# Seven-part product 3, LayerNorm sums on ScalarE, and an earlier order of small work, in a two-layer linear-attention and GLU kernel

## The chip, the cores and the metric

One core of one Trainium2 chip. The metric is the device time of one execution in microseconds (us). Besides the time, each run has a span, from its first to its last instruction; it is 1.7 to 2.1 us shorter than the time.

## The reference, cut to what matters

```python
# x: 2048 x 1024; wqkv: 1024 x 3072; w_gate, w_up: 1024 x 3584; w_down: 3584 x 1024; bf16
x = x + A(layernorm(x))      # linear attention, 32 heads
x = x + B(layernorm(x))      # B(x) = ((x @ w_gate) * (x @ w_up)) @ w_down
x = x + A(layernorm(x))      # the same weights again
x = x + B(layernorm(x))
```

## The kernel before

Large products are made from seven smaller ones, numbered 1 to 7, of sums of quarter matrices (the Strassen scheme in a form with eight sums, S1 to S4 of one operand and T1 to T4 of the other). Each of the two layers has two passes of gate/up and "down", a pass for each half of the tokens. Within "down" some of the seven products are split once more, into seven parts with sums of their own; `L2DOWN` says which, and `DSCHED` after which group of matmuls each sum is put on VectorE.

```python
L2DOWN = {(False, 0): "45", (False, 1): "5", (True, 0): "45", (True, 1): "453"}   # (second layer?, pass): split products
DSCHED = {
    ...
    "5": {"20": "S1:5", "21": "S2:5", "22": "S3:5", "23": "S4:5", "41": "T1:5", "42": "T2:5", "43": "T3:5", "5d": "T4:5"},
    "453": {... "5d": "T4:5 S4:3", "5h": "T1:3", "5k": "S3:3", "5m": "T2:3", "3d": "T3:3", "3f": "T4:3"},
}
```

Every operation names the pages that it reads and writes, and the program works out its waits from that; each engine runs its operations in the order of the program. LayerNorm of a tile of 128 tokens takes its sums on VectorE (`ln_a`) or, for five tiles of the first LayerNorm, on ScalarE in two steps (`ln_s1`, `ln_s2`) with a little GpSimd arithmetic after each; then comes the standardisation (`ln_b2`) and a transposing DMA from SBUF to SBUF. The standardised tile lies in a buffer:

```python
def dst(self, n):                      # buffer of the n-th tile
    if self.to == "A0":
        return xrt[n], r_xr(n)
    o = (O_XN + [O_WQ])[n % 3] if self.to == "B" and n < 14 else O_XN[n % 2]    # B: three in turn, two for the last tiles
    return vh(o, D), R(o, D * 2)

def start(self, i, mid=None):
    if self.to == "A0" and i in LN_ACT:
        j = ln_s1(self.order[i], *self.dst(i))       # ScalarE: sum
        self.q_s.append((i, j))                      # squares follow in s2()
    else:
        j = ln_a(self.order[i], mid)                 # VectorE: bn_stats, bn_aggr
    ...

def lnstep(i, h):                      # first projections, one tile behind another
    if h == 0:
        ...
        if lnp.n < NST:
            lnp.start(lnp.n)
        lnp.b_one()
    else:
        lnp.s2()
        ...

def p7(c):                             # gate/up: bank of product 7, copied, then the multiply of the finished quarter
    pe("7", c, X[c], False)
    cp(1, c, X[c])
    c22(c)
```

Of the kernel before, what the change touches and what calls it, by code (L numbers as in the profile page):

```python
# [180 lines left out]
def build_kernel(nc, A_x, A_wqkv, A_wo, B_w_gate, B_w_up, B_w_down, out):  # L181
    _, S, D = A_x.shape
# [20 lines left out]
    ORDER0 = "D3A' P1A P7B' P6A D2B' 51 D4B' D3B' R0 56 D2A P1B T0 P7A 57 P5A W P6B T1 D4A R0 P5B S5+"  # L203
    ORDER1 = "P5A' 47' T0 P7B' D4A' P5B' 11 D3A' R0 51 16 D4B' D2B' P1A 17 T1 56 D3B' P6A P1B 41 R0 57 S5+ S2+ D2A P6B 46 P7A"
    ORDER2 = "11 57' D2B' P7B' 16 T0 P5A' 21 D4B' P1A 17 S2+ D3A' P5B' 26 R0 P6A D2A S5+ 41 27 P1B D3B' 46 51 T1 P7A 47 P6B 56 D4A R0"
    L2DOWN = {(False, 0): "45", (False, 1): "5", (True, 0): "45", (True, 1): "453"}
    DSCHED = {
        "45": {"20": "S1:5 S1:4", "21": "S2:5 S2:4", "22": "S3:5 S4:4", "23": "S4:5", "70": "S3:4 T1:4", "72": "T2:4 T3:4", "73": "T1:5",
               "4d": "T4:4", "4j": "T2:5", "4m": "T3:5", "5d": "T4:5"},
        "5": {"20": "S1:5", "21": "S2:5", "22": "S3:5", "23": "S4:5", "41": "T1:5", "42": "T2:5", "43": "T3:5", "5d": "T4:5"},  # L210
        "453": {"20": "S1:5 S1:4", "21": "S2:5 S2:4", "22": "S3:5 S4:4", "23": "S4:5", "70": "S3:4 T1:4", "71": "S1:3", "72": "T2:4 T3:4", "73": "T1:5",
                "4d": "T4:4", "4f": "S2:3", "4j": "T2:5", "4m": "T3:5", "5d": "T4:5 S4:3", "5h": "T1:3", "5k": "S3:3", "5m": "T2:3", "3d": "T3:3", "3f": "T4:3"},
    }
    ORDERS = {(False, 0): ORDER0, (False, 1): ORDER1, (True, 0): ORDER2, (True, 1): ORDER2}
    SZ_W = KT * D * 2
# [109 lines left out]
    with ExitStack() as es:  # L325
# [13 lines left out]
        def vh(o, n):  # L339
            return ah[:, o // 2: o // 2 + n]  # L340
# [158 lines left out]
        class LN:  # L499
# [13 lines left out]
            def dst(self, n):  # L513
# [2 lines left out]
                o = (O_XN + [O_WQ])[n % 3] if self.to == "B" and n < 14 else O_XN[n % 2]  # L516
                return vh(o, D), R(o, D * 2)

            def start(self, i, mid=None):
                assert i == self.n  # L520
                if self.to == "A0" and i in LN_ACT:
                    j = ln_s1(self.order[i], *self.dst(i))
                    self.q_s.append((i, j))
                else:
                    j = ln_a(self.order[i], mid)
                self.n += 1
                self.q_b.append((i, j))

            def s2(self, upto=NST):
                while self.q_s and self.q_s[0][0] <= upto:  # L530
                    i, j = self.q_s.pop(0)
                    ln_s2(self.order[i], j, *self.dst(i))

            def b1_one(self):
                if self.q_b:
# [368 lines left out]
        def layer_A(lnp, nxt, first):  # L904
# [173 lines left out]
            def lnstep(i, h):  # L1078
                if h == 0:
                    if first and lnp.n < NST:  # L1080
                        for t in range(lnp.n, lnp.n + 5):
                            if xnext[0] <= t < NST:
                                xload(t)
                                xnext[0] = t + 1
                    if lnp.n < NST:
                        lnp.start(lnp.n)
                    lnp.b_one()
                else:
                    lnp.s2()
                    lnp.use_dma = i + 1 >= NPE_T  # L1090
                    lnp.step_t(1)
# [20 lines left out]
                seq += [("q", i - NHOLD - 1), ("k", i)]  # L1112
            seq += [("q", i) for i in range(max(NPL - NHOLD - 1, 0), NPL if NPL < NST else 0)]
            mids = {("k", 2, 0): lambda: None}
            lead = [[], [lambda: lnp.step_t(1)], [lambda: lnp.start(4)], [lambda: lnp.b_one(), lambda: lnp.start(5)]]
            if first:
                (p0, e0_), (p1_, e1_) = [proj("k", tok[0], h, "parts") for h in range(2)]
                (pt1, et1), (pt1b, et1b) = [proj("k", tok[1], h, "parts") for h in range(2)]
# [259 lines left out]
        def layer_B(lnp, nxt, first):  # L1378
# [10 lines left out]
            def pair(ps_, p, l2):  # L1389
# [66 lines left out]
                def p7(c):  # L1456
                    pe("7", c, X[c], False)
                    cp(1, c, X[c])
                    c22(c)

                def p5(c):
                    if "5" in L:
# [2 lines left out]
                        pe("5", c, Y[c], True)  # L1465
                    c22(c)

                ORDER = [q[0] for q in ORDERS[not first, ps_].split() if q[0] in "1245" and q[1] == "1"]

                def l2_of(q):  # L1470
# [103 lines left out]
                def fin(q, c):  # L1574
# [4 lines left out]
                        pe(q, c, bank, False)  # L1579
                    add = L[q]["s"](c) if q in L and q in "24" else cpb(0, c) if q == "3" else None  # L1580
                    return lambda: mul(c, {"2": "1", "4": "4", "3": "3"}[q], bank, add)
                return dict(p1=p1, p5=p5, p6=p6, p7=p7, L=L, fin=fin, sums=sums)

            def gateup(ps_, ticks, l2):
                jit = first and ps_ == 0
# [28 lines left out]
                                return  # L1614

                def emit(p, tk, head=False):
                    if tk[-1] == "'":
                        p, tk = p - 1, tk[:-1]
                    if p < 0 or (p == 0 and not head and tk in pre):
                        return  # L1620
                    if p == 1 and tk[0] in l2 and tk[1] == "1":
                        tp_next(tk[0])
                    c, x = pairs[p], "AB".find(tk[-1])
                    if tk[0] == "P":
                        c["p" + tk[1]](x)
                    elif tk[0] == "D":
                        c["fin"](tk[1], x)()
                    elif tk[0] in "1245":
                        step(p, tk[0], int(tk[1]))
                    elif tk[0] == "R":  # L1630
                        if p or tk == "R1":
                            ring_issue()
                    elif tk == "W":
                        wd_dma()
                    elif tk[0] == "S" and not (early and p == 0):
                        sums(p + (tk[2] == "+"), tk[1])
                    elif tk[0] == "T":
                        i = int(tk[1])
                        if jit:
                            store_s(n0 + 2 * p + i)  # L1640
                            if p + 1 < NP:
                                prep_s(n0 + 2 * p + 2 + i)
                        ticks(2 * p + i)
                    if p == 0 and tk in ("P1B", "P5B", "D2B", "D4B") and tk[1] in l2:
                        plain.add(tk[1])
                    if p == 0 and not head:
                        tp_next()
# [32 lines left out]
            def down(ps_, ticks, tail):  # L1680
# [12 lines left out]
                    i = i0 + 4 * sh + t  # L1693
                    return x_res[:, i, d * 512:(d + 1) * 512], r_x(i, d * 512, (d + 1) * 512)

                def final(sh, d, t):
                    i = i0 + 4 * sh + t
                    if is_last:
                        xs, rx = xq(sh, d, t)
                        dma(out2[i * 128:(i + 1) * 128, d * 512:(d + 1) * 512], xs, [], KOUT, rd=rx)  # L1700

                def hblk(q, kh, mh):
                    hv, ho = hs[q]
# [12 lines left out]
                    return xnT[:, 0:7, c0:c0 + 256], _seg(O_XT, 7, S * 2, c0 * 2, (c0 + 256) * 2)  # L1716

                tr, ha_ = [flat(O_T + 3584 * i) for i in range(3)], [flat(O_HA + 3584 * i) for i in range(4)]
                sbuf2 = {"4": [xbuf(i) for i in range(3)], "5": tr if "4" in l2d else [xbuf(1 + i) for i in range(3)], "3": [xbuf(i, 1 - ps_) for i in range(3)]}
                tbuf2 = {"4": [flat(RE), flat(RE + 3584), flat(O_XN[0])], "5": [xbuf(3) if "4" in l2d else ha_[2], ha_[0], ha_[1]], "3": [ha_[2], ha_[3], xbuf(3, 1 - ps_)]}  # L1720
                r4 = [(vf(o, 512), R(o, 2048)) for o in (RC, RC + 2048, RB + 28672, RB + 30720)]
                l2w = {}
                for q in l2d:
# [17 lines left out]
                def run_l2(q, evac):  # L1741
# [49 lines left out]
                    def m7(r):  # L1791
                        mm(7, r, UB[r], 1)
                        if q == "5":
                            put5(r + 2, r)
                            put(r + 2, r)
                        else:
                            acc(r + 2, 1, r, 1, rout)
                            acc(r + 2, 0, r, 1, rin)

                    def m2(r):  # L1800
                        mm(2, r, DB[r], 0)
# [4 lines left out]

                    def m4(r):
                        mm(4, r, DB[r + 2], 0)
                        evac(r + 2)
                    f = first_  # L1810
                    order = ((f, 0), (f, 1), (m2, 0), (m6, 0), (m2, 1), (m6, 1), (m7, 0), (m3, 0), (m7, 1), (m3, 1), (m4, 0), (m4, 1))
                    for st_, (fn, r) in enumerate(order):
                        fn(r)
                        if st_ == 9:
                            ring_issue()
                            ring_issue()
                        l2_ops(q, "abcdefghijkm"[st_])

                tail(0)
                for qi, q in enumerate(DPROD):  # L1820
# [106 lines left out]
            def dticks1(q, t):  # L1927
                if is_last:
                    return
                if q != "3":  # L1930
                    nxt.step_t(1)
                    nxt.b2_one()
                    nxt.b1_one()
                    if t % 2 == 0 and nxt.n < 8:
                        nxt.start(nxt.n)
                if q == "1" and t == 3:
                    for c in (1, 2, 4):
                        tw_load("k", c)
                if q == "7" and t == 3:
                    for c in (2, 4):  # L1940
                        tw_load("q", c)
                if q == "5":
                    s_make(nxt.order, 0)[t]()
                if q == "5" and t == 3:
                    for w in "kq":
                        load_w(w, 0)
                        t, v, c0, base = WSRC[w]
                        dma(t[:, 4:8, 512:1024], v[:, 4:8, c0 + 512:c0 + 1024], _seg(base + 4 * D * 2, 4, D * 2, 1024, 2048), KW[w][1])
                        tw_load(w, 3)
                    tw_load("q", 1)  # L1950
                if q == "3":
                    stash(12 + t)
                    nxt.step_t(1)
                    nxt.b2_one()
                    nxt.b1_one()
                    nxt.start(8 + t)
                    if t == 3:
                        for k in range(4):
                            stash(8 + k)
# [81 lines left out]
```

## Time and profile before

| | before |
|---|---|
| time, median of 3 (range) | 1434.42 us (1434.38 to 1434.63) |
| span of the profiled run | 1432.5 us |
| TensorE busy | 99% |
| VectorE, ScalarE, GpSimd busy | 84%, 48%, 10% |
| the waits of TensorE that the prediction lists, from start to start | 6.0 us in all |

The prediction shows the lines behind this.

### The profile page before, as it was taken

How to read it: one execution, taken by the hardware profiler on the slowest of the kernel's cores; microseconds unless marked ns; L12 is line 12 of the kernel's file. 1: busy time of each engine (PE TensorE's matmuls, PEld its weight loads, DVE VectorE, ACT ScalarE, POOL GpSimd, SP SyncE). 2: the span in 40 equal slices, each digit the busy share in tenths (PEclk: the TensorE clock that was granted, in tenths of full speed). 3: DMA queues (queue and kind: packets, MB, share of what 16 DMA engines can do in the span).
4: the chain of work that ended last, by engine and by line, in shares of the span. 5: the costliest groups of instructions: out<-in, count | busy, mean ns of one | idle time of the engine just before them, and what ended most of it. 6: DMA issues, size and time to landing. Idle time of an engine off the chain costs nothing.

```text
span 1432.5 us, 21777 instructions
## 1 busy us (share of the span) xinstructions
PE 1420.4 (99%) x8107; PEld 786.5 (55%) x8167; DVE 1210.1 (84%) x2371; ACT 687.8 (48%) x1409; POOL 148.5 (10%) x181
## 2 busy tenths in 40 slices
PE   9999999999999999999999999999999999999999
PEld 4444444555546566664544444446666475666547
DVE  6897878999988799988679978778888887888888
ACT  5882355444410266652157814667766004767400
POOL 2203521000010000002000045300000100000000
PEclk9999999999999999999999999999999999999999
DMA  7868979997786777768793366767775976777653
GB/s 231 208 141 230 222 173 199 305 308 265 253 265 215 228 258 249 251 227 308 225 291 92 90 173 167 176 187 254 260 246 193 292 254 225 259 259 260 204 192 120
DMA packets 270554, 320.73 MB, mean 224 GB/s; under 512 B 164080, under 2 KB 210928, under 8 KB 270448
## 3 DMA queue, kind: packets, MB, share of 16 engines
q1 hardware_dynamic: 270448, 319.34, 72.9%
q8 instruction: 64, 1.05, 0.3%
q14 instruction: 42, 0.34, 0.1%
HBM read 236.45 MB, written 73.40 MB: 216 GB/s over the span
## 4 chain that ended last, share of the span: by engine, by line
PE 86%; DVE 8%; ACT 2%; issue 2%; DMA 1%; POOL 1%; SPq 0%; POOLq 0%; DVEq 0%
PE ps L1414 28%; PE ps L1495 17%; PE ps L1831 14%; PE ps L1230 8%; PE ps L1332 6%; PE ps L970 6%; PE ps L1749 5%; DVE arena L802 4%; DVE arena L454 1%; PE ps L943 1%; DVE arena L805 1%; DMA arena<-arena 1%; DVE arena L649 1%; ACT arena L662 1%; PE ps L1256 1%
## 5 line engine op out<-in xcount | busy, mean ns | idle before, releaser
L802 DVE TENSOR_TENSOR arena<-arena 128x512 f16<-128x512 f16 (+9 forms) x1019 | 499.2, 518 | 59.5 <-ACT arena L1499 34.1
L1414 PE MATMUL ps<-arena 128*128 128x512 f16 x1888 | 457.0, 379 | 0.5 <-DVE arena L805 0.4
L805 DVE SCALAR_TENSOR_TENSOR arena<-ps,arena 128x512 f16<-128x512 f32 (+3 forms) x545 | 353.9, 664 | 67.5 <-PE ps L1831 28.4
L1495 PE MATMUL ps<-arena 128*128 128x256 f16 x2184 | 287.6, 273 | 1.0 <-DVE ps L1508 1.0
L1414 PEld LDWEIGHTS ps<-arena 128*128 128x128 f16 (+1 forms) x1888 | 182.9, 98 | 162.9 <-ACT ps L1443 3.8
L1495 PEld LDWEIGHTS ps<-arena 128*128 128x128 f16 (+1 forms) x2184 | 212.0, 98 | 91.9 <-ACT arena L1499 7.1
L1831 PE MATMUL ps<-arena 128*128 128x512 bf16 (+1 forms) x1102 | 242.6, 379 | 0.9
L1831 PEld LDWEIGHTS ps<-arena 128*128 128x128 f16 x1120 | 109.5, 98 | 130.3 <-DVE arena L802 0.3
L1419 ACT ACTIVATE arena<-ps 128x512 f32<-128x512 f32 x224 | 133.8, 597 | 76.4 <-PE ps L1414 61.6
L1499 ACT ACTIVATE arena<-ps 128x256 f32<-128x256 f32 x351 | 125.1, 384 | 26.9 <-PE ps L1495 22.0
L970 PE MATMUL ps<-arena 128*128 128x512 f16 (+1 forms) x606 | 134.1, 379 | 1.1 <-ACT arena L977 0.4
L1230 PE MATMUL ps<-arena 128*128 128x512 bf16 x498 | 114.7, 379 | 0.7
L1332 PE MATMUL ps<-arena 128*128 128x512 bf16 x502 | 110.3, 379 | 0.5
L459 POOL TENSOR_SCALAR arena<-arena 128x1 f32<-128x1 f32 x59 | 20.8, 353 | 805.4 <-DVE arena L458 805.4
L1505 ACT COPY ps<-ps 128x256 f32<-128x256 f32 x182 | 66.3, 364 | 75.4 <-DVE arena L805 30.0
L970 PEld LDWEIGHTS ps<-arena 128*128 128x128 f16 x616 | 59.5, 98 | 74.7 <-ACT arena L977 5.8
L1443 ACT COPY ps<-ps 128x512 f32<-128x512 f32 x112 | 65.4, 584 | 63.2 <-PE ps L1414 51.9
L1072 POOL TENSOR_TENSOR arena<-arena 128x1024 f16<-128x1024 f32 x32 | 77.0, 2405 | 155.9 <-DVE arena L1070 142.6
L1749 PE MATMUL ps<-arena 128*128 128x256 f16 (+1 forms) x784 | 86.7, 273 | 0.7 <-DVE arena L805 0.5
L454 DVE BATCH_NORM_STATS2 arena<-arena 128x6 f32<-128x512 bf16 x118 | 81.2, 688 | 5.0 <-DMA arena<-in_A_x_dram 3.0
L1508 DVE TENSOR_TENSOR ps<-ps,arena 128x256 f32<-128x256 f32 x182 | 76.7, 428 | 10.3 <-PE ps L1495 9.4
L1332 PEld LDWEIGHTS ps<-arena 128*128 128x128 f16 x512 | 50.1, 98 | 60.4
(72 smaller groups left out, 939.8 us busy)
## 6 DMA issues: line engine op xcount, KB each, us to landing
arena<-w_scratch SPq DMA_DIRECT2D x84, 896.0 KB, 4.5
arena<-t_scratch SPq DMA_DIRECT2D x32, 896.0 KB, 5.7
arena<-in_B_w_down_dram SPq DMA_DIRECT2D x24, 896.0 KB, 5.1
arena<-sp_scratch SPq DMA_DIRECT2D x26, 768.0 KB, 4.3
w_scratch<-arena SPq DMA_DIRECT2D x28, 512.0 KB, 6.1
arena<-w_scratch SPq DMA_DIRECT2D x28, 384.0 KB, 4.9
x_scratch<-arena SPq DMA_DIRECT2D x40, 256.0 KB, 7.3
arena<-x_scratch SPq DMA_DIRECT2D x40, 256.0 KB, 5.8
```

The costliest lines, as they stand in the source:

```text
L454: P.add("dve", (lambda h: lambda e: e.bn_stats(st[j][:, 6 * h:6 * h + 6], x_res[:, i, (D // 2) * h:(D // 2) * (h + 1)]))(h), rd=r_x(i, (D ...
L802: P.add("dve", lambda e: e.tensor_tensor(out=out, in0=a, in1=b, op=op), rd=rd, wr=wr, prd=prd)
L805: P.add("dve", lambda e: e.scalar_tensor_tensor(out=out, in0=a, scalar=sc, in1=b, op0=ALU.mult, op1=op1), rd=rd, wr=wr, prd=prd)
L970: P.add("pe", lambda e: [e.matmul(psb(bank), a[0][:, k, :], b[0][:, k, :], start=(q in (1, 5) and k == 0), stop=(k == 3), skip_group_check ...
L1230: return [e.matmul(psb(bank), xrt[t][:, jj * 128:(jj + 1) * 128], pk[:, h, t, :], start=(t == tok[0]), stop=(t == tok[NST - 1])) for t in ts]
L1332: return [e.matmul(psb(bank), xnT[:, g, i * 128:(i + 1) * 128], wp[:, g, dh * 512:(dh + 1) * 512], start=(dh == 0 and g == 0), stop=(g == ...
L1414: P.add("pe", lambda e: [e.matmul(psb(bank), w[:, k, :], x[:, k, :], start=(start and k == 0), stop=(k == 3), skip_group_check=True) for k ...
L1419: P.add("act", lambda e: e.activation(t, psb(bank), AF.Copy, scale=SG), prd=[bank], wr=r)
L1495: P.add("pe", lambda e: [e.matmul(psb(bank)[:, 256 * half:256 * half + 256], w[:, k, :], xx[:, k, :], start=(start and k == 0), stop=(k == ...
L1499: P.add("act", lambda e: e.activation(d, src, AF.Copy, scale=sc), prd=[xk], wr=rd_)
L1749: P.add("pe", lambda e: [e.matmul(psb(bank)[:, 256 * half:256 * half + 256], a[:, k, 128 * r:128 * r + 128], b[:, k, :], start=(start and ...
L1831: P.add("pe", lambda e: [e.matmul(psb(bank), hv[:, 7 * hf + k, t * 128:(t + 1) * 128], w[:, k, :], start=(q in "15" and hf == 0 and k == 0 ...
```

## The change

The intent: less TensorE work in product 3 of the first layer's second down pass; VectorE, which has to make the sums for that, relieved of LayerNorm's sums; and four places where small work stands in TensorE's way put in another order. The diff, cut to its core:

```diff
-    L2DOWN = {(False, 0): "45", (False, 1): "5", ...}
+    L2DOWN = {(False, 0): "45", (False, 1): "53", ...}
-        "5": {...}
+        "53": {... "40": "S1:3", ... "5b": "S2:3", "5d": "T4:5", "5f": "S3:3", "5i": "T1:3", "5m": "T2:3", "3b": "T3:3", "3d": "S4:3", "3f": "T4:3"},
         "453": {...
-                ... "5d": "T4:5 S4:3", "5h": "T1:3", "5k": "S3:3", "5m": "T2:3", "3d": "T3:3", "3f": "T4:3"},
+                ... "5b": "S3:3 S4:3", "5d": "T4:5", "5f": "T1:3", "5i": "T2:3", "5m": "T3:3", "3b": "T4:3"},
@@ LayerNorm sums of twelve tiles to ScalarE (its output goes to a scratch buffer, junk)
-                if self.to == "A0" and i in LN_ACT:
-                    j = ln_s1(self.order[i], *self.dst(i))
+                if self.to == "A0" and i in LN_ACT or self.to == "A" and i < 12:
+                    j = ln_s1(self.order[i], *self.junk(i))
@@ first projections: squares of the tile before go ahead of the next tile's sums; tile 4 a step earlier
+                    lnp.s2()
                     if lnp.n < NST:
                         lnp.start(lnp.n)
-            lead = [[], [lambda: lnp.step_t(1)], [lambda: lnp.start(4)], [lambda: lnp.b_one(), lambda: lnp.start(5)]]
+            lead = [[], [lambda: lnp.step_t(1), lambda: lnp.start(4)], [lambda: lnp.b_one()], [lambda: lnp.start(5)]]
@@ gate/up: the first pair's multiply is put off (emitted later, in the pass's order)
-                    c22(c)
+                    if p or not later:
+                        c22(c)
@@ last product: last tile evacuated and stored in halves
+                        if is_last and q == "3" and r:
+                            half3(r + 2, 0)
+                            return
                         evac(r + 2)
@@ next LayerNorm beside product 3: four tiles' sums in eight half steps
+                if q == "3s":
+                    if t < 8:
+                        nxt.s2() if t % 2 else nxt.start(8 + t // 2)
```

## The prediction

> **What bounds the kernel now.** I read the busy shares first, then what the TensorE waited for, then the places of those waits in the timeline, and last the chain at the end.
>
> ```profile
> PE 1420.4 (99%) x8107; PEld 786.5 (55%) x8167; DVE 1210.1 (84%) x2371; ACT 687.8 (48%) x1409; POOL 148.5 (10%) x181
> ```
>
> TensorE is the bound, nearly everywhere. The program has 8167 matmuls; 8107 were recorded, so a start-to-start distance that is one matmul too long with an idle time of 52 or 53 ns before it is a missing record, not a wait, and I leave those out. Time can come off in two ways only: less TensorE work, or fewer of the few waits. These are most of the waits (who waited for whom, us in total, times, longest):
>
> ```profile
> PE ps L943 <- ACT arena L662: 1.1, 2, 0.7
> PE ps L1495 <- DVE ps L1508: 1.0, 2, 0.5
> PE ps L943 <- DMA arena<-arena: 0.6, 1, 0.6
> PE ps L1749 <- DVE arena L805: 0.5, 1, 0.5
> PE ps L970 <- ACT arena L977: 0.4, 2, 0.2
> PE ps L1749 <- ACT ps L1762: 0.2, 1, 0.2
> ```
>
> A shown matmul lasts 379 ns (512 columns) or 273 ns (256), but successive ones start 216 or 109 ns apart, so each listed wait costs 0.16 us more than its gap. I therefore count waits from start to start: 0.75 us at 31.12 and 0.90 us at 38.93 (first projections), 0.20, 0.53 and 0.21 us at 56 to 69 us, 0.33, 0.29 and 0.36 us at 745 to 788 us (second layer's projections), 0.66 us each at 958.75 and 1201.01 (first pairs of the second layer's gate/up), 0.62 us at 1159.02, 0.39 us at 1417.86 and 0.15 us at 1424.89. Some others (start of the program, 243.68) are not touched.
>
> The TensorE timeline around the product that is to be split, in the first layer's second down stage:
>
> ```profile
> 706.45 10.86 PE L1749 MATMUL ps<-arena 128*128 128x256 f16 x98
> 717.36 12.03 PE L1831 MATMUL ps<-arena 128*128 128x512 bf16 x54
> 729.23 15.70 PE L970 MATMUL ps<-arena 128*128 128x512 bf16 x71
> ```
>
> The first line is product 5, already in seven parts: 98 matmuls of 256 columns. The second is product 3, still whole: 56 of 512 columns (two not recorded).
>
> **What the Trainium skill says.** "TensorE: Matmul & The Clock Gate", section "Back-to-back issue gap", gives N/2.4 + 2.5 ns warm: 109 ns for 256 columns, 216 ns for 512. The trace agrees: 10.86 us less one shown duration of 0.273, over 97 steps, is 109.1 ns. The same section's 131 ns per 512-column matmul in a sustained stream isn't seen here. "Perfetto Trace Analysis", section "Tensor Engine Instruction (MATMUL, LD_WEIGHTS)", says that matmul ends are estimated and that ScalarE, VectorE and GpSimd are strict FIFO; the wait below shows that order. "VectorE: DVE Perf Modes", section "The perf-mode tier table", has 16-bit tensor_tensor at twice the rate and operands in PSUM at the single one: here 1082 ns for 1792 elements of f16, 420 ns for 256 out of PSUM. "DMA: Bandwidth & Descriptors", section "Anatomy of one DMA — SWDGE (gpsimd) path", puts some 2 us of fixed cost on a DMA; here the last stores of 128x512 take 1.7 us from issue to landing, on the SyncE queue, so halving a store should win little.
>
> **The change part by part.**
>
> *Product 3 in seven parts.* Removed: 56 x 215.8 ns = 12.08 us. Added: 98 x 109.2 ns = 10.70 us. Gain 1.38 us on TensorE, certain if no operand is late. Its price is on VectorE: eight sums of 128x1792 at about 1.0 us from start to start = 8.0 us, and fourteen 256-column accumulations for one less 512-column evacuation in net count over the program (the last tile's halves account for two of those), some 5 us more. Paid by taking LayerNorm's sums of twelve tiles off VectorE: 12 x (2 x 0.69 + 0.21) = 19 us less. They go to ScalarE: 12 x (1.07 + 1.15) plus accumulator reads = 31 us, where it was busy 6.0, 5.8 and 2.8 us in the three 25-us stretches from 650. I walked product 3's VectorE queue with the durations above: its operands are ready 0.5 us or more ahead of every part, so I expect no wait inside it.
>
> *The start.* This is the wait at 38.93 and its root:
>
> ```profile
> 31.27 0.21 POOL L459 TENSOR_SCALAR arena<-arena 128x1 f32<-128x1 f32 x1 [3.42 <-DVE arena L458]
> 31.57 0.57 POOL L465 TENSOR_TENSOR arena<-arena 128x1 f32<-128x1 f32 x1
> 32.20 0.19 POOL L480 TENSOR_SCALAR arena<-arena 128x1 f32<-128x1 f32 x1
> 32.48 0.56 POOL L465 TENSOR_TENSOR arena<-arena 128x1 f32<-128x1 f32 x1
> 33.07 0.55 DVE L495 TENSOR_SCALAR arena<-arena 128x1024 f16<-128x1024 bf16 x1 [1.88 <-POOL arena L465]
> 34.31 0.60 ACT L662 ACTIVATE arena<-ps 128x512 f16<-128x512 f32 x1 [2.75 <-DVE arena L802]
> ```
>
> GpSimd's L480 belongs to tile 5, whose squares ScalarE had ready at 29.13. It stood behind L459 of tile 6, whose statistics ended at 31.2. VectorE then sat 1.88 us for tile 5, and ScalarE 2.75 us for VectorE, while a PSUM bank stayed full. The order of the built program has L480 ahead of L459 now, so the standardisation can start at about 31.2 and all behind it comes some 2 us sooner; 0.90 us should go. Tile 4's statistics also move ahead of a 1.2-us weight difference: its transpose was issued at 27.84 and landed at 31.12, for a TensorE free at 30.37. Issued at about 26.6, and with the same 3.3 us, it lands before that: 0.75 us more. Gain 1.64 us. The three later waits of this stage have other roots (the same GpSimd order for other tiles) and stay.
>
> *First pairs of gate/up.*
>
> ```profile
> 957.20 0.69 DVE L805 SCALAR_TENSOR_TENSOR arena<-ps,arena 128x512 f16<-128x512 f32 x1 [0.47 <-ACT arena L1419]
> 957.92 0.42 DVE L802 TENSOR_TENSOR arena<-arena 128x512 f16<-128x512 f16 x1
> 958.26 0.42 DVE L1508 TENSOR_TENSOR ps<-ps,arena 128x256 f32<-128x256 f32 x1
> 958.75 0.83 PE L1495 MATMUL ps<-arena 128*128 128x256 f16 x6 [0.49 <-DVE ps L1508]
> ```
>
> The multiply (L805, L802) stands ahead of the addition L1508 that TensorE needs. With the multiply put off L1508 can start when its matmuls end, about 957.35, and is done by 957.8, when TensorE needs it at 958.1. Gain 2 x 0.66 = 1.31 us. The third pass that gets the same order had no such wait.
>
> *The last product and tile.*
>
> ```profile
> 1416.07 1.00 DVE arena L802
> 1417.07 0.35 DVE ps L1765
> 1417.44 0.37 ACT ps L1762
> 1429.06 1.32 DVE arena L805 x2
> ```
>
> This is the chain at the end. L802 is a sum of the last product standing ahead of L1765, a PSUM addition that TensorE waits for. With the sums moved to places where VectorE is free I find no wait left: 0.39 + 0.15 = 0.54 us. The last evacuation of 512 columns (0.69 us, ending at 1430.38 after a TensorE end of 1429.65) becomes one of 256 (0.42): 0.3 us. Together 0.85 us.
>
> *Second layer's projections.* Here the change costs. In product 3 ScalarE now sums four tiles, each about 3.02 us (sum, GpSimd's sign, squares; the start at 34.80 to the next free start at 37.82). From 716.05 that is 12.1 us, then one standardisation of 1.14: ScalarE is free at 729.3. But the first pair's bank copy, 0.57 us, is wanted by 729.74 on the shortened clock (product 3 ends at 728.0, two groups of four follow). I expect a wait of 0.2 us. Two standardisations move from ScalarE (1.24 us each) to VectorE (0.53): that takes away the 0.33-us wait at 745.10, but from 750 on VectorE has no idle time (24.2 of 25 us busy), and one of the two falls there: 0.3 us. Net loss 0.2 us.
>
> Sum: 1.38 + 1.64 + 1.31 + 0.85 - 0.2 = 5.0 us; 1434.42 - 5.0 = 1429.4, and I take 1429.5.
>
> **Rivals.** (1) *The gain is only arithmetic.* The waits taken away come back a little later, because VectorE at 84% or ScalarE is the real pace there; the three small waits at 56 to 69 us speak for it, VectorE's 1.9-us idle time against. Then 1.4 us of product 3, 0.85 of the end and half of the rest remain: 1431. (2) *ScalarE becomes the bound at the turn from down to projections.* The sums of four tiles, one after the other through GpSimd, run past the first copies. If each takes 3.5 us the wait is 2 us and more: 1431.5. For it: 12.1 us of chain in 12 us of room. Against: ScalarE is otherwise idle there. (3) *A transfer is late.* The query weights were issued from 715.7 to 722.3 and landed as late as 732.30; in the new clock the second group of the second item wants them at about 733.0. The margin of 0.7 us is small, and a slip costs that slip: up to 1 us. (4) *Relief of VectorE helps more than I count:* the 0.29- and 0.36-us waits go too: 1428.7.
>
> **Range and chances.** The parts that are simple arithmetic or local order (2.7 us: product 3 and first pairs) are nearly sure; the end (0.85) likely; the start (1.64) and the turn (-0.2) are each uncertain by about 0.7 us. Runs of the kernel before lie within 0.25 us. That gives 1428.3 to 1431.0. Two per cent is 28.7 us, six times all that is at stake: 99% for within 2%, and half a per cent for each side, for a fault that I haven't seen.
>
> **What would show it right or wrong.** Product 3 as 98 matmuls of 256 in 10.7 us without a wait; L480 ahead of L459 and no waits at 31 and 39 us; no waits of TensorE for L1508's line at the heads of the two passes; the last store issued about 0.6 to 1.0 us after the last matmul. Wrong: a new wait of more than 0.5 us on the first copies after product 3, waits at 55 to 70 us grown by what was saved before them, or VectorE late for the split product.

## More of the kernel before

```profile
q1 hardware_dynamic: 270448, 319.34, 72.9%
q8 instruction: 64, 1.05, 0.3%
```

Queue 8 brings 64 packets of 16 KB, 1.05 MB, none of it data.

## The result, and the profile after

Ratios here are the mean time of one kernel's runs over that of the other's runs of the same rounds, so not quite the ratio of the medians that are quoted.

The changed kernel takes 1430.53 us (median of 4, 1430.10 to 1431.05), the kernel before in the same rounds 1434.53 us (1434.38 to 1435.08): ratio 0.9972, 95% interval 0.9954 to 0.9989. That is 4.0 us faster where 5.0 was predicted, inside the range and within 2%. All outputs are right.

The busy shares after, and TensorE's waits after (who waited for whom, us in total, times, longest):

```profile
PE 1421.5 (99%) x8209; PEld 790.0 (55%) x8209; DVE 1205.5 (84%) x2356; ACT 712.5 (50%) x1455; POOL 154.5 (11%) x193
```

```profile
PE ps L1854 <- DVE arena L806: 1.7, 1, 1.7
PE ps L435 <- POOL arena L431: 1.4, 1, 1.4
PE ps L974 <- ACT arena L981: 0.6, 3, 0.2
PE ps L1761 <- DVE arena L809: 0.5, 1, 0.5
```

Gone from the list are the two at the first pairs of gate/up, those of the first projections and those of the last product. Its first line is new, and is the largest of all: L1854 (before: L1831) is the down stage's product.

Product 3 of the first layer on TensorE's timeline:

```profile
704.59 21.56 PE L1761 MATMUL ps<-arena 128*128 128x256 f16 x196
725.99 9.28 PE L974 MATMUL ps<-arena 128*128 128x512 bf16 x42
```

Products 5 and 3 are now one run of 196 matmuls of 256 columns, 109.2 ns apart, with no wait inside it and none when the projections begin.

GpSimd at the start of the program:

```profile
28.82 0.45 POOL L481 TENSOR_SCALAR arena<-arena 128x1 f32<-128x1 f32 x1 [1.36 <-ACT arena L479]
31.55 0.56 POOL L460 TENSOR_SCALAR arena<-arena 128x1 f32<-128x1 f32 x1 [1.63 <-DVE arena L459]
```

The step of tile 5 (L481, before L480) now runs at 28.8 us, ahead of that of tile 6, where it stood behind it until 32.2.

The new wait, on VectorE's and TensorE's timelines in the second layer's first down stage. First before, then after:

```profile
1122.91 0.55 DVE L495 TENSOR_SCALAR arena<-arena 128x1024 f16<-128x1024 bf16 x1 [4.43 <-DMA arena<-arena]
1140.17 2.21 DVE L802 TENSOR_TENSOR arena<-arena 128x1792 f16<-128x1792 f16 x2
1120.69 25.63 PE L1831 MATMUL ps<-arena 128*128 128x512 bf16 x117
```

```profile
1121.04 0.55 DVE L496 TENSOR_SCALAR arena<-arena 128x1024 f16<-128x1024 bf16 x1 [6.31 <-DMA arena<-arena]
1138.30 2.21 DVE L806 TENSOR_TENSOR arena<-arena 128x1792 f16<-128x1792 f16 x2
1140.57 1.68 PE L1854 MATMUL ps<-arena 128*128 128x512 f16 x7 [1.66 <-DVE arena L806]
```

The first line is the standardisation of tile 14. It writes a buffer that tile 12 used, and so waits until tile 12's transpose has landed: VectorE sat 4.43 us before the change and 6.31 us after. TensorE had reached this down stage 3.75 us sooner and the transpose was issued 3.9 us sooner, but it landed only 1.9 us sooner. From there VectorE runs with one pause of 0.46 us to L806, a sum for product 6, which is late by what the transpose was late: TensorE waits 1.83 us from start to start. In the kernel before, the same sum ended at 1142.38, just in time: TensorE's 117 matmuls there follow each other without a gap.

### The profile page after: what moved, and what is told of

The parts are those of the page before. It is cut to its first block, busy times and chain, and to the rows that moved or that the text cites. A ratio compares the mean times of both kernels' runs of the same rounds, so it can differ in the third digit from the quotient of the medians. Undisturbed runs are those within 1.5% of the kernel's fastest.

```text
span 1429.3 us, 21974 instructions
## 1 busy us (share of the span) xinstructions
PE 1421.5 (99%) x8209; PEld 790.0 (55%) x8209; DVE 1205.5 (84%) x2356; ACT 712.5 (50%) x1455; POOL 154.5 (11%) x193
## 4 chain that ended last, share of the span: by engine, by line
PE 86%; DVE 7%; issue 2%; ACT 2%; POOL 1%; DMA 1%; SPq 0%; POOLq 0%; DVEq 0%
PE ps L1419 28%; PE ps L1502 17%; PE ps L1854 13%; PE ps L1235 8%; PE ps L974 8%; PE ps L1761 6%; PE ps L1337 4%; DVE arena L806 3%; DVE arena L455 2%; PE ps L947 1%; DMA arena<-arena 1%; DVE arena L809 1%; POOL arena L466 1%; PE ps L1261 1%; PE ps L1288 0%
## 5 line engine op out<-in xcount | busy, mean ns | idle before, releaser
L806 DVE TENSOR_TENSOR arena<-arena 128x512 f16<-128x512 f16 (+7 forms) x1027 | 507.2, 522 | 57.2 <-ACT arena L1506 32.7
L809 DVE SCALAR_TENSOR_TENSOR arena<-ps,arena 128x512 f16<-128x512 f32 (+3 forms) x558 | 358.4, 658 | 76.8 <-PE ps L1854 36.8
L1854 PE MATMUL ps<-arena 128*128 128x512 bf16 (+1 forms) x1064 | 232.6, 379 | 1.7 <-DVE arena L806 1.7
L1854 PEld LDWEIGHTS ps<-arena 128*128 128x128 f16 x1064 | 103.8, 98 | 125.9 <-DVE arena L806 2.2
L974 PEld LDWEIGHTS ps<-arena 128*128 128x128 f16 x616 | 59.3, 98 | 74.9 <-ACT arena L981 5.8
L1761 PE MATMUL ps<-arena 128*128 128x256 f16 (+1 forms) x882 | 97.2, 273 | 0.5 <-DVE arena L809 0.5
L1761 PEld LDWEIGHTS ps<-arena 128*128 128x128 f16 x882 | 86.0, 98 | 11.9 <-DVE arena L809 1.0
L1337 PEld LDWEIGHTS ps<-arena 128*128 128x128 f16 x512 | 50.0, 98 | 60.5
L1789 ACT COPY arena<-ps 128x256 f32<-128x256 f32 x8 | 3.0, 372 | 158.3 <-PE ps L1761 158.3
```

The source lines that it names most:

```text
L806: P.add("dve", lambda e: e.tensor_tensor(out=out, in0=a, in1=b, op=op), rd=rd, wr=wr, prd=prd)
L809: P.add("dve", lambda e: e.scalar_tensor_tensor(out=out, in0=a, scalar=sc, in1=b, op0=ALU.mult, op1=op1), rd=rd, wr=wr, prd=prd)
L974: P.add("pe", lambda e: [e.matmul(psb(bank), a[0][:, k, :], b[0][:, k, :], start=(q in (1, 5) and k == 0), stop=(k == 3), skip_group_check ...
L1337: return [e.matmul(psb(bank), xnT[:, g, i * 128:(i + 1) * 128], wp[:, g, dh * 512:(dh + 1) * 512], start=(dh == 0 and g == 0), stop=(g == ...
L1761: P.add("pe", lambda e: [e.matmul(psb(bank)[:, 256 * half:256 * half + 256], a[:, k, 128 * r:128 * r + 128], b[:, k, :], start=(start and ...
L1854: P.add("pe", lambda e: [e.matmul(psb(bank), hv[:, 7 * hf + k, t * 128:(t + 1) * 128], w[:, k, :], start=(q in "15" and hf == 0 and k == 0 ...
```

## The experiments

Twelve runs in three batches of four, each batch on one chip together with the kernel before, whose medians there were 1435.09, 1435.12 and 1434.46 us. Where a kernel of the second or third batch is called so much slower than after_buf or faster than the changed kernel, which ran in other batches, that difference goes across chips, and 0.6 us of it can be the batch's. The intervals of the ratios are some 0.0013 to each side, wider than most differences here, because the runs of the kernel before spread over up to 2.7 us. (Part of it is the start of the program: in the profiles TensorE gets to its second group of projections at 16.1 to 18.1 us, by how soon the first weights land.)

### Again, and with a third buffer

Is the late transpose what holds TensorE, and is it an accident of one run?

> The changed kernel once more, on the chip that the other three of this batch share, to see how far its wait of 1.8 us in the second layer's first down stage (product 6) repeats. If that wait is set by when a transpose happens to land, its size differs here by some tenths of a us to 2 us and the time with it (1430.0 to 1431.1). If it belongs to the change, it is there at 1.8 us in every run and the spread stays as small as the kernel before's 0.25 us.

> The kernel before as it is, for a second trace. If the landing of the transposes of tiles 12 and 13 scatters from run to run whatever the kernel, this trace has another landing time than the 6.6 us of the first, and where it is over 8 us a wait in product 6 as in the changed kernel; if the change makes it late, it is 6.6 us again and there is no such wait. Time 1434.4 to 1435.1.

> The changed kernel with a third buffer for the normalised tile 14 of the layer B, so that VectorE need not wait for the transpose of tile 12 before it writes tile 14. Theory 1 (a late transpose holds VectorE, VectorE's sums then come late for product 6): VectorE's idle time of 6.3 us ahead of that write goes, TensorE's waits of 1.8 us in product 6 and 0.66 us in product 4 go, 1428.0 to 1428.8 us, and the runs lie within 0.3 us. Rival (VectorE has too much to do in this stage anyway): its idle time goes, but the 0.66-us wait in product 4 stays, and the gain is under 1 us.

> The kernel before with the same third buffer. Theory 1: its 0.62-us wait in product 4 of the same stage goes, 1433.8 us; the wait isn't of the change's making, only nearer to the edge. Rival (VectorE has too much to do): same time as before, within 0.2 us.

The edit of the two `_buf` kernels gives tile 14 a buffer (and a semaphore) of its own, so that it doesn't wait for tile 12's transpose:

```diff
                 o = (O_XN + [O_WQ])[n % 3] if self.to == "B" and n < 14 else O_XN[n % 2]
+                if self.to == "B" and n == 14:
+                    o = RE
@@ semaphore of the transpose
-KTL[n % (3 if self.to == "B" and n < 14 else 2)]
+KTL[2 if self.to == "B" and n == 14 else n % (3 if self.to == "B" and n < 14 else 2)]
```

| kernel | median us (runs) | ratio to before | wait at product 6, us | tile 12's transpose, issue to landing, us |
|---|---|---|---|---|
| after_again | 1430.99 (1430.59 to 1431.17) | 0.9973 | 1.46 | 8.34 |
| after_buf | 1428.85 (1428.74 to 1429.34) | 0.9959 | none | 8.16 |
| before_again | 1434.56 (1434.05 to 1435.16) | 0.9999 | none | 6.05 |
| before_buf | 1433.81 (1433.25 to 1435.03) | 0.9996 | none | 6.12 |

With the third buffer the wait is gone and the changed kernel is 2.1 us faster; a wait of 0.66 us in the following product 4, which the kernel before had too (0.62, and 0.32 in before_again), goes with it. (VectorE still waits 1.80 us there in after_buf, now for tile 13's transpose, and TensorE waits for none of it.) So the late transpose does hold VectorE, and the rival, that VectorE simply has too much to do there, falls. But my other idea, that the landing scatters by chance from run to run, falls as well: it is 8.2 to 8.6 us in all three changed kernels and 6.05 to 6.6 us in all three others. Something in the change, which alters nothing in this stage, makes the transpose land 2 us later.

### One part of the change undone at a time

All on top of after_buf, whose time is not blurred by the wait. The landing of the transpose was to tell which part makes it late.

**u_start** puts the first projections' order back (no squares' step ahead of the next sums; tile 4 where it was).

> The changed kernel with the third buffer, and the start's order of before (tile 4's statistics a step later, no squares' step ahead of the next tile's sums). My theory: both waits come back (0.75 us near 31, 0.90 near 39 us) and nothing later takes them up again, so it is 1.6 to 2.1 us slower than the same kernel without the undoing (ratio to before 0.9971 to 0.9974 instead of 0.9959). Rival: the first layer's later waits (63, 242 us) take half of it up: 0.8 to 1.0 us slower (0.9965). Landing time of tile 12's transpose in the second layer: I expect the 8.2 to 8.6 us of the other changed kernels, as this part lies 1080 us ahead of it.

1430.67 us (1430.54 to 1432.39), ratio 0.9972, 1.8 us slower. Waits of 0.46 (as in before_again, not 0.75) and 0.91 us are back at 31.2 and 39.1 us, and 0.19 and 0.53 us at 56.5 and 64.0, where after_buf has one of 0.13. Transpose: 7.71 us. My theory held, with one thing more: of the two later waits the change takes away all but 0.13 us.

**u_pair** puts the multiply of the first pairs back.

```diff
-                    if p or not later:
-                        c22(c)
+                    c22(c)
```

> The changed kernel with the third buffer, and the gate/up multiply of first pairs where it was. My theory: the waits of 0.66 us each come back at the heads of the second layer's two gate/up passes (near 954 and 1197 us): 1.3 us slower, ratio to before 0.9968. Rival: the multiply put off is only paid later in the same pass, so undoing it costs under 0.5 us. Landing time of tile 12's transpose: if the put-off multiply is what makes it late, it goes from 8.2 or more to 6.1 to 6.6 us here, and stays at 8.2 or more in the other three runs.

1430.41 us (1429.88 to 1430.95), ratio 0.9968. The two waits are back with 0.65 and 0.66 us, at 956.2 and 1197.8. As predicted; the transpose, 7.50 us, stays late, so my guess that this part makes it late falls.

**u_p3** makes product 3 whole again, with the sums left on ScalarE, put beside the four groups of product 3.

> The changed kernel with the third buffer, and product 3 of the first layer's second down stage whole again (56 matmuls of 512 columns), with the LayerNorm sums left on ScalarE. My theory: arithmetic of TensorE alone: 1.38 us slower, ratio to before 0.9968 to 0.9969. Rival: the split product's sums cost VectorE something that shows in the second layer's projections (three waits of 0.36 us); then undoing it costs only 0.3 to 0.7 us, and some of those waits go. Landing time of tile 12's transpose: 8.2 to 8.6 us.

1431.97 us (1431.65 to 1432.45), ratio 0.9979: 3.1 us slower, twice what I expected. TensorE's timeline at the turn to the projections, and ScalarE's:

```profile
731.18 2.12 PE L975 MATMUL ps<-arena 128*128 128x512 f16 x9 [0.94 <-ACT ps L978]
```

```profile
729.40 1.24 ACT L492 ACTIVATE arena<-arena 128x1024 f16<-128x1024 bf16 x1 [3.47 <-DVE arena L486]
730.55 0.58 ACT L978 COPY ps<-ps 128x512 f32<-128x512 f32 x1
```

Here ScalarE is late with the first copy, L978, because a standardisation stands before it: a wait of 1.10 us. That is rival 2 of the prediction, but in this kernel and not in the changed one, because my undoing starts the four sums later than the change's eight half steps. So 1.4 us of the 3.1 are product 3 and 1.1 are my undoing's own. The rest lies, in the profiles, in two places that the edit does not touch: TensorE got to its second group of projections 0.5 us later, and a wait near 243 us (0.83 us in after_buf) is 1.00. The transpose lands after 6.43 us: early again.

**u_ln** puts the LayerNorm sums of the twelve tiles back on VectorE and keeps product 3 in seven parts.

> The changed kernel with the third buffer, product 3 in seven parts, but the LayerNorm sums of the twelve tiles on VectorE again. My theory: VectorE has no room for both in the down stage, so TensorE waits within it or at the turn to the projections: 2 to 4 us slower, ratio to before 0.9973 to 0.9987, the waits in product 3, in those just ahead of it or in the first projection groups. Rival: VectorE's slack carries it, and the move to ScalarE buys nothing: within 0.5 us, perhaps faster by 0.3 us as ScalarE's path at the turn goes. Landing time of tile 12's transpose: 8.2 to 8.6 us.

1434.66 us (1434.59 to 1436.49), ratio 0.9999: 5.8 us slower, more than I expected. TensorE's timeline in product 3 and just after:

```profile
723.05 0.94 PE L1763 MATMUL ps<-arena 128*128 128x256 f16 x7 [0.30 <-DVE arena L811]
725.91 1.94 PE L1763 MATMUL ps<-arena 128*128 128x256 f16 x14 [1.92 <-DVE arena L811]
728.77 3.23 PE L1763 MATMUL ps<-arena 128*128 128x256 f16 x28 [0.92 <-DVE arena L811]
735.35 1.90 PE L976 MATMUL ps<-arena 128*128 128x512 f16 x8 [1.63 <-ACT ps L979]
```

VectorE (L811 accumulates product 3's parts) has no room for both. From start to start the waits are 3.9 us in product 3 and 1.8 us at the turn. (The profile is of the slowest run, 1436.49 us, which lost another 1.5 us before the second group of projections.) The relief by ScalarE is not an extra: without it the split product 3 loses more than it gains. Transpose: 7.72 us.

So of the four, only the kernel with product 3 whole lands the transpose early, though product 3 ends 390 us before that transpose is issued.

### What joins the two: TensorE's own instructions

The DMA queues in the stretch from the first of the eight loads ahead of the transpose to its landing, first in the kernel before, then in the changed one (the first row is the busy share of the 16 DMA engines in 40 slices of the stretch, in tenths):

```profile
DMA  9999989889998899999999999999999999299999
...
q1 hardware_dynamic: 3762, 3.95, 108.8%
q14 instruction: 1, 0.01, 0.2%
```

```profile
DMA  9999487979899999999999999999960995000999
...
q1 hardware_dynamic: 3810, 3.94, 115.3%
q8 instruction: 1, 0.02, 0.5%
q14 instruction: 1, 0.01, 0.2%
```

The second has a packet of queue 8 and the first has none, and near its end the second has three slices, 1.0 us, in which the DMA engines do almost nothing although the transpose has not landed. The Trainium skill, "Runtime: NRT & Kernel Launch", section "Instruction fetch mechanics", says that an engine's instructions are fetched while it runs, in blocks of 16 KiB, 256 instructions, over a DMA queue that its sequencer drives. The trace agrees: 64 packets of 16,384 bytes, for 2 x 8167 = 16,334 matmuls and weight loads, one each 22 us; and the next experiment, which touches no engine but TensorE, moves them. Product 3 in seven parts has 42 matmuls more, 84 instructions with their weight loads, so all later packets are wanted a third of a period earlier: before the change packets start at 1103.3 and 1131.3 us, with the transpose under way from 1116.19 to 1122.81; after it one starts at 1118.3, with the transpose under way from 1112.33 to 1120.94. That packet took 1.18 us.

Two kernels shift the packets and nothing else, by issuing some 512-column matmuls of the first layer's first down stage as two of 256 columns:

```diff
-    [e.matmul(psb(bank), ..., w[:, k, :], ...) for k in range(7)]
+    parts = ((0, 256), (256, 512)) if first and ps_ == 0 and (COND) else ((0, 512),)
+    [e.matmul(psb(bank)[:, lo:hi], ..., w[:, k, lo:hi], ...) for k in range(7) for lo, hi in parts]
# before_shift42: COND is  q == "2" and t < 3              (42 matmuls, 84 instructions more)
# after_shift84:  COND is  q == "2" or q == "6" and t < 2  (84 matmuls, 168 instructions more)
```

> The kernel before, with 42 of the 512-column matmuls of the first layer's first down stage issued as two of 256 columns: the same sums, 84 more instructions for TensorE (as many as the split of product 3 adds), no other engine touched. My theory: TensorE's instructions come in packets of 16 KB over the same DMA engines, and 84 instructions more move the packet that was fetched at 1131 us to about 1122, on top of the transpose of tile 12 in the second layer. Then the transpose lands 7.5 to 8.6 us after its issue instead of 6.05 to 6.6, a wait of 1.2 to 1.8 us appears near 1144 us in product 6, and the kernel is 1.3 to 1.9 us slower (0.1 us of it for the extra matmuls): ratio 1.0009 to 1.0013. Rival: it is something else in the split of product 3 that makes the transpose late; then it lands after 6.05 to 6.6 us, no wait appears, ratio 1.0001.

1436.11 us (1435.64 to 1436.92) beside 1434.46 us (1434.07 to 1435.63) of the kernel before: ratio 1.0010, 1.65 us slower; its fastest run is as slow as the slowest of the kernel before. Its packet starts at 1120.9 us and takes 1.92 us; the transpose lands 8.09 us after its issue. The same lines as above, of this kernel (DMA queue in the stretch, VectorE, TensorE):

```profile
q8 instruction: 1, 0.02, 0.9%
```

```profile
1124.65 0.55 DVE L495 TENSOR_SCALAR arena<-arena 128x1024 f16<-128x1024 bf16 x1 [5.74 <-DMA arena<-arena]
1144.17 2.12 PE L1832 MATMUL ps<-arena 128*128 128x512 f16 x9 [1.08 <-DVE arena L802]
```

The kernel before has got the changed kernel's wait, 1.25 us from start to start, with no engine's work changed but the cutting of 42 matmuls.

> The changed kernel as it is, without the third buffer, with 84 matmuls of the first layer's first down stage issued as two of 256 columns: 168 more instructions for TensorE, with the 84 of the change 252, so that the packets of 256 instructions fall almost where they fell before the change. My theory: the packet near 1118 us goes to about 1100 and the next to about 1128, the transpose of tile 12 lands 6.0 to 6.6 us after issue, the wait of 1.5 to 1.8 us near 1140 is gone or under 0.3 us (a wait of 0.6 us near 1157 stays), and in spite of 0.2 us for the extra matmuls it is 1.2 to 1.6 us faster than the changed kernel: ratio to before 0.9961 to 0.9964 instead of 0.9972. Rival: landing after 8.2 us or more, and 0.2 us slower than the changed kernel, 0.9974.

1429.43 us (1428.90 to 1430.11), ratio 0.9964, where the changed kernel has 0.9972 and 0.9973. The packets start at 1100.7 and 1127.9 us, the transpose lands after 6.37 us, the wait is gone (that of 0.6 us near 1157, which I expected to stay, is 0.31):

```profile
1119.44 0.55 DVE L496 TENSOR_SCALAR arena<-arena 128x1024 f16<-128x1024 bf16 x1 [4.13 <-DMA arena<-arena]
```

```profile
1116.66 25.63 PE L1855 MATMUL ps<-arena 128*128 128x512 bf16 x117
```

One run of 117 matmuls where the changed kernel had a gap. With 84 matmuls more it is 1.1 to 1.6 us faster. All 14 profiles side by side:

| profile | packet starts | transpose, issue to landing | us |
|---|---|---|---|
| before; again; with buffer | 1103.3, 1131.3 (the two others within 0.6) | 1116.2 to 1122.8 | 6.62; 6.05; 6.12 |
| u_p3 | 1103.2, 1130.5 | 1115.7 to 1122.1 | 6.43 |
| u_p3ln | 1101.5, 1128.8 | 1114.3 to 1120.6 | 6.28 |
| after_shift84 | 1100.7, 1127.9 | 1113.0 to 1119.4 | 6.37 |
| after; again; with buffer | 1118.3; 1117.4; 1117.0 | 1112.3 to 1120.9 | 8.61; 8.34; 8.16 |
| u_start | 1119.1 | 1114.6 to 1122.3 | 7.71 |
| u_pair | 1117.8 | 1113.4 to 1120.9 | 7.50 |
| u_ln | 1124.5 | 1119.7 to 1127.5 | 7.72 |
| u_end | 1117.8 | 1112.5 to 1121.0 | 8.53 |
| before_shift42 | 1120.9 | 1116.5 to 1124.6 | 8.09 |

Wherever the packet starts while the transpose is under way, it lands after 7.5 us or more, and elsewhere within 6.62. In the three profiles that have the wait (after, after_again, before_shift42), it is about the landing less 6.8 us: 1.83, 1.46 and 1.25.

### The other parts

**u_p3ln** undoes product 3 and the move of the sums together.

> The changed kernel with the third buffer, and both product 3 whole again and the LayerNorm sums of the twelve tiles on VectorE again, as before the change. What the two are worth together: my theory is the 1.38 us of the predicted sum and next to nothing at the turn to the projections (0.2 us), so 1.2 to 1.5 us slower than with them: ratio to before 0.9968 to 0.9970. Rival: they cost more at the turn than I see, then under 1.0 us slower. The transpose of tile 12 lands after 6.05 to 6.6 us, as product 3 is whole.

1430.22 us (1430.07 to 1430.44), ratio 0.9969: 1.4 us slower. As expected: 1.38 us of TensorE work, and next to nothing at the turn.

**u_end** puts the last product's schedule and the whole last tile back.

> The changed kernel with the third buffer, and the last product's sums and the last tile as before the change. The prediction gave 0.54 us for two waits in that product and 0.3 us for the last tile in halves, 0.85 in all: ratio to before 0.9965 instead of 0.9959. Rival, from the stages of the profiles read so far: the halves bring 0.18 us, and the stage 0.3 to 0.5 us, so 0.5 to 0.7 us slower: ratio 0.9963.

1429.66 us (1429.23 to 1430.48), ratio 0.9965: 0.8 us slower. The waits of 0.39 and 0.15 us are back, at 1413.1 and 1420.1. From TensorE's end to the program's end it is 2.87 us here and 2.68 in after_buf. So the halves bring 0.19 us, not 0.3.

The best version is after_buf: 1428.85 us, 2.1 us less than the changed kernel in the same batch.

## Why the prediction was right, and where not

| term of the sum | predicted, us | measured, us | from |
|---|---|---|---|
| product 3 | -1.38 | -1.38 | 98 x 109.2 ns in the place of 56 x 215.8 ns, no wait |
| start | -1.64 | -2.1 (-2.3 again) | length of this stage on TensorE, 51.22 before, 49.13 after (48.91 again) |
| first pairs | -1.31 | -1.31 | both waits gone; back in u_pair |
| last product | -0.54 | -0.46 | both waits gone, back in u_end; one of 0.07 is new at 1425.70 |
| last tile | -0.3 | -0.18 | TensorE's end to the program's end, 2.86 and 2.68 |
| second layer's projections | +0.2 | +0.1 | no wait at the turn; three waits of 0.98 in all become 1.07 |
| down stage of the second layer | 0 | +1.8 (+1.5 again) | instruction packet on the transpose |
| sum | -5.0 | -3.5 to -4.1 | medians: -4.0 |

- **The local terms were right.** Each wait that was traced to an order of instructions went when the order was changed, and came back with the order. "No waits at 31 and 39 us", product 3 "without a wait" and "no waits of TensorE for L1508's line" all came true.
- **The start was undersized.** The prediction said that three later waits (0.94 us) "have other roots (the same GpSimd order for other tiles) and stay". But the change puts the squares' step ahead for every tile of that stage, not for one. Of the three, the 0.20 at 56 us went and the 0.53 at 64 us shrank to 0.29 (0.10 in the second profile); the third, 0.21 at 69 us, lies after the stage and stayed. With 0.75 and 0.90 that makes the 2.09 us. The 0.75 itself is 0.46 in before_again and before_shift42, so part of that term is one run's.
- **The turn.** The expected wait of 0.2 us for the first copy did not come; the three waits of 0.36 us in the projections, where there were 0.33, 0.29 and 0.36, cost 0.1. As forecast, the 0.33 at 745 went and another, of 0.35, came (at 766.12). Rival 2 did not happen. u_p3, where the same sums start later and TensorE waits 1.10 us, shows that the margin was small.
- **The last tile was oversized by 0.1 us.** The last store was issued 0.60 us after TensorE's end instead of 0.76, and landed 1.65 us later instead of 1.69. I had counted the whole difference of two evacuations (0.69 and 0.42 us).
- **What the prediction failed to see.** Its sum has no term for stages that the change doesn't touch. Rival 3, "a transfer is late", was of the right kind, but in the wrong place (query weights near 733 us) and for another reason. The step that failed is the assumption behind "Time can come off in two ways only": that whatever isn't edited moves up as a whole. TensorE's instruction packets do not move with the program; they follow the count of its instructions. Here the 42 matmuls added in product 3 put one on a transpose with 0.2 us of slack (it landed after 6.62 us; up to 6.8 would have done). That the total still fell within the range is in part luck: this cost 1.5 to 1.8 us, and the start, undersized by 0.5 to 0.7, gave some of it back.
- **Open.** Which of the 16 DMA engines carries the packet is not recorded, and why a packet of 0.9 to 1.9 us makes the transpose up to 2.6 us later is not shown. The three empty slices above say that the DMA engines wait then, rather than being full, and the packet records say for what they could be waiting: between 1119.0 and 1120.0 us of the changed kernel only 19 packets start, all of the transpose's 256-byte kind and none before 1119.45, when the instruction packet is about to end (1119.48); from 1120.25 on some 250 GB/s flow again. All eight profiles with the packet on the transpose have such a stretch, 1.1 to 2.0 us with under 3 kB started in each tenth of a us; the six others have none. That the 19 are the share of the one engine that was busy with the packet, and that the others wait for it, is argued, not shown.

## What to carry to other kernels

Adding instructions to the engine that is the bound can cost time hundreds of us later, in a stage that is not edited: look for transfers with little slack (a buffer reused as soon as a transpose lands), and compare issue-to-landing times of the same transfer in both profiles before blaming the stage. A third buffer for that one tile is a cheap cure, and is worth more than tuning the phase of the packets, which the next edit shifts again. When work is moved off an engine to make room, test the room by moving it back: here the split without the relief was 5.8 us slower.

## What the Trainium skill lacked or had wrong

- "Runtime: NRT & Kernel Launch", section "Instruction fetch mechanics", calls the cost of crossing a 16-KiB block "mostly hidden". For TensorE itself nothing here speaks against it: every wait in the lists above has another engine or a transfer behind it. It lacks that the packet can delay a data transfer on the same DMA engines: a transpose that lands 6.05 to 6.62 us after its issue took 7.5 to 8.6 us with a packet (0.9 to 1.9 us) during it, which cost 1.25 to 1.83 us of the program where no third buffer hid it.
- "TensorE: Matmul & The Clock Gate", section "Back-to-back issue gap": the 131 ns per 512-column matmul of a sustained stream was not seen; 56 matmuls in a row were 215.8 ns apart, and 196 of 256 columns 109.2 ns.
- No page that I found gives the time of an SBUF-to-SBUF transpose of 128 x 1024 two-byte elements issued behind 2 MB of loads: 6.05 to 6.62 us here, and about 3.1 us for a transpose issued a few us later without such loads ahead of it.
